# Attention, a soft mixture of experts and an MLP on one core: a conversion that ends sooner, K/Q tiles that later hold weights, and second weights with two rows to a partition

## Chip, cores and metric

The kernel runs on one core of a Trainium2 chip. The metric is device time in microseconds (us), the median of three runs. The core has TensorE (PE, matrix products), VectorE (DVE), ScalarE (ACT), GpSimd (POOL), and SyncE (SP), whose queue issues nearly all DMA transfers.

## What is computed

```python
# q, k, v: (4, 12, 448, 64); x: (1792, 768); float32, w_in and w_out arrive as float64
scores = cap * tanh(q @ k.T / sqrt(64) / cap)          # per batch and head
x = concat_heads(softmax(scores) @ v)                   # (4*448, 768)
logits = x @ phi                                        # 32 slots: 8 experts x 4
d = softmax(logits, axis=tokens); c = softmax(logits, axis=slots)
slot_in = (d.T @ x).reshape(8, 4, 768)
slot_out[e] = relu(slot_in[e] @ w1[e]) @ w2[e]          # w1: (8,768,1024), w2: (8,1024,768)
x = c @ slot_out
h = x @ w_in                                            # (768, 2048)
out = (max(h, 0) + alpha * min(h, 0)) @ w_out           # (2048, 768)
```

## The kernel before

**Three stages in a row.** `attention()` works on 24 pairs of heads (i), four steps each (g = 4i + c): a step computes a chunk of the scores on PE (`qk`), tanh and exp on ACT, and, two steps later, the product with V (`pv`). In the steps with g mod 4 = 1 `pv` ends a pair: ACT copies the PSUM tile o to xu (L413), and the next pair's first V product waits for that copy, since o has one buffer. In the same steps K and Q of the next pair are transposed (`trans_k`, `trans_q`) from the natural K and Q tiles, two buffers of 4 KB a partition in the pools `nat0` and `nat1`. Background work (row sums, normalisation, logits, both softmaxes) is put into later steps by `later`. `softmax_c` runs for each batch once its logits are transposed, the last one behind the loop.

**W_in's conversion** turns float64 into float32 in 24 pieces during attention: one DMA in, one ACT instruction (L184), four on DVE (L185 to L195), one DMA to a scratch tensor. `cv_steps` gives the steps: 4, 7, ... 25, 29 and then every fourth step up to 89. The last piece is stored at step 91, and only then the buffer `cvbuf` (slot 10 of the weight arena) becomes free for weights.

**Expert weights** come as 32 entries in consumption order, four to an expert: two halves of w1 and two of w2, 1.57 MB each. Entries 0 to 9 are loaded into arena slots during attention (steps in `LOADS`), entry 10 into slot 10 after the conversion, entries 11 to 17 in parts into the extra slots (L114), which lie where the attention's pools were, so that each part waits until its predecessor there is free; entry 11 has one part loaded early. Entries 18 and on go into arena slots as the experts leave them (L163). Entries 18, 19, 22, 23, 26, 27, 31, 32 are halves of w2. All loads are issued by SP in this order; w_in's and w_out's follow behind the last expert. A half of w1 is one DMA with 12 KB a row run, one of w2 four DMAs with 3 KB runs.

**The experts stage** (`experts`) does for each expert, on PE: h = slots x w1 (L823; 24 products of 256 columns, four at a time on column groups), two transposes of relu(h) (L837, behind ACT's relu, L834), y += hT x w2 (L845; 24 products of 256 columns, three at a time). An fp32 product shows as two MATMUL records. `build_c` makes the second softmax's operand behind experts 5 and 6, `split_wo(0)` starts w_out's conversion at expert 7 (DVE L185 to L195, L793).

**The MLP stage**: `gather` transposes y (DVE ysb L863), `a_block` multiplies with w_in, `project` does the output products (L954 to L961).

The tile framework keeps data dependences by itself and may place a ready instruction ahead of one that waits, within an engine.

Of the kernel before, what the change touches and what calls it, by code (L numbers as in the profile page):

```python
# [24 lines left out]
def tile_attention_soft_moe_mlp(ctx, tc, q, k, v, cap, phi, w1, w2, w_in, w_out, alpha, out):  # L25
# [29 lines left out]
    LOADS = (2, 4, 6, 8, 10, 12, 14, 16, 18, 20, 21, 22)  # L55
# [16 lines left out]
    c_all = const.tile([P, B, J, NSLOT], F32, name="c_all")  # L72
# [3 lines left out]
    early = [arena.tile([128, SLOT // 4], F32, tag=f"early{c}", name="w") for c in range(QE)]  # L76

# [29 lines left out]

    def load_part(kind, e, i, c, t, after=None):
        if kind == "w2":
            o = 512 * i + 128 * c  # L110
            src = w2[e, o:o + 128, :]
# [121 lines left out]
    def attention():  # L233
        with ExitStack() as pools:
# [3 lines left out]
            nat_0 = pool("nat0")  # L238
            nat_1 = pool("nat1")
# [18 lines left out]
            nat_p, stk_p, v_p, acc_p = (nat_0, nat_1), (stk_0, stk_1), (v_0, v_1), (acc_0, acc_1)  # L258
# [13 lines left out]
            ktails = [nat_p[n].tile([128, 2, D], F32, tag="kt", name="kt") for n in range(2)]  # L272
# [39 lines left out]
            def load(i, names):  # L312
# [3 lines left out]
                for nm in names:  # L316
                    src = {"k": k, "q": q, "v": v}[nm][b, 2 * m:2 * m + 2]

                    if nm == "q":
                        t = nat_p[i % 2].tile([P, J, 2, D], F32, tag=nm, name=nm)  # L320
# [4 lines left out]
                    elif nm == "k":  # L325
                        t = nat_p[i % 2].tile([128, 2 * JK, D], F32, tag=nm, name=nm)
# [264 lines left out]
            def nat_last(ls, fo):  # L591
                ps = aux([P, J * NSLOT], "nd")
                for j in range(J):
                    transpose(
                        ps[:, j * NSLOT:(j + 1) * NSLOT], ls[0:NSLOT, j * P:(j + 1) * P], ident[:NSLOT, :NSLOT]
                    )
                dl[B - 1] = sm_p.tile([P, J, 64], F32, tag="dl", name="dl")
                nc.vector.tensor_copy(out=dl[B - 1][:, :, 0:NSLOT], in_=ps.rearrange("p (j s) -> p j s", j=J))
# [9 lines left out]
            def nat_d(b, ls, fo):  # L608
# [3 lines left out]
                dl[b] = sm_p.tile([P, J, 64], F32, tag="dl", name="dl")  # L612
                nc.vector.tensor_copy(out=dl[b], in_=ps.rearrange("p (j s) -> p j s", j=J))
                later(1, softmax_c, b)
# [30 lines left out]
            def softmax_c(b):  # L645
                lg = dl[b][:, :, NSLOT:2 * NSLOT]
                mx = sm_p.tile([P, J, 1], F32, tag="mx", name="mx")
                sm = sm_p.tile([P, J, 1], F32, tag="sm", name="sm")
                ce = c_all[:, b]
                bc = [P, J, NSLOT]  # L650
                nc.vector.reduce_max(out=mx, in_=lg, axis=AX.X)
                nc.vector.tensor_sub(out=ce, in0=lg, in1=mx.to_broadcast(bc))
# [4 lines left out]
                nc.vector.tensor_mul(out=c_all[:, b], in0=ce, in1=sm.to_broadcast(bc))  # L657

            craw, cout = {}, {}
            cvbuf = slot(NA - 1, [128, 3, 1024], U32, name="cvbuf")  # L660

            def load_w_in(i):
# [4 lines left out]
                nc.sync.dma_start(out=craw[i], in_=w_in[kk * 128:(kk + 1) * 128, fb * 512:(fb + 1) * 512, :])  # L667
# [5 lines left out]
            while len(cv_steps) < ncv:  # L673
                cv_steps.append(cv_steps[-1] + J)
# [39 lines left out]
            for g in range(NPAIR * J + LAG):  # L714
# [4 lines left out]
                if g == 17:  # L719
                    nc.vector.tensor_scalar(out=nalpha_sb, in0=alpha_sb, scalar1=-1.0, scalar2=None, op0=ALU.mult)  # L720
# [5 lines left out]
                run_bg()  # L726
                if i < NPAIR:
# [40 lines left out]
            softmax_c(B - 1)  # L768

    def tail():  # L770
# [27 lines left out]
        def build_c(b, cve_p, ps_w, cstk):  # L798
# [5 lines left out]
            ps = ps_w.tile([128, 512], F32, tag="w", name="tc")[:, :S]  # L804
# [6 lines left out]
        G3 = DM // 256  # L811

        def experts(which, ex2_p, ps_w, yacc, cv_p=None, cstk=None):
            for e in which:
# [4 lines left out]
                h1 = ps_w.tile([128, 512], F32, tag="w", name="h1")[:, :256]  # L819
                for kk in range(KD):  # L820
                    wv = where["w1", e, kk // 3]
                    for j in range(4):
                        nc.tensor.matmul(  # L823
                            h1[32 * j:32 * j + 32, :],
                            slotT[:, kk, :],
                            wv[kk % 3][:, 256 * j:256 * j + 256],
                            start=(kk == 0),
                            stop=(kk == KD - 1),
                            tile_position=(0, 32 * j),
                        )  # L830
                done_with("w1", e, 0)
                done_with("w1", e, 1)
                rl = ex2_p.tile([128, 256], F32, tag="rl", name="rl")
                nc.scalar.activation(out=rl, in_=h1, func=AF.Relu)  # L834
                tp = ps_w.tile([128, 512], F32, tag="w", name="tp")[:, :256]
# [17 lines left out]
                done_with("w2", e, 0)  # L853
                done_with("w2", e, 1)
                if EH <= e < EH + B // 2:
                    for b in (2 * (e - EH), 2 * (e - EH) + 1):
                        build_c(b, cv_p, ps_w, cstk)

        def gather(ps_w, yacc, cv_p, so):
            warm = ps_c.tile([128, 512], F32, tag="c", name="warm")  # L860
            idle(2, warm)
            ysb = cv_p.tile([128, DM], F32, tag="ct", name="ysb")[:32 * G3, :256]
            nc.vector.tensor_copy(out=ysb, in_=yacc[:32 * G3, :256])  # L863
            yt = ps_w.tile([128, 512], F32, tag="w", name="yt")[:, :64 * G3]
            for u in range(2):
                pe[0] = nc.tensor.transpose(
                    yt[:, 32 * G3 * u:32 * G3 * (u + 1)], ysb[:, 128 * u:128 * u + 128], ident[:32 * G3, :32 * G3]
                )
            idle(3, warm)
            for r in range(2):  # L870
                dst = so[:, :, r, :].rearrange("p (g u) s -> p u g s", u=2)
                src = yt.rearrange("p (u g s) -> p u g s", u=2, g=G3)
                nc.vector.tensor_copy(out=dst, in_=src)
# [151 lines left out]
        with (  # L1025
# [3 lines left out]
            with tc.tile_pool(name="ex2", bufs=1, reuse_waits="tile", side="right") as ex2_p:  # L1029
                yacc = ps_c.tile([128, 512], F32, tag="c", name="y")  # L1030
                with tc.tile_pool(name="xtra", bufs=1, reuse_waits="tile") as xt_p:
# [3 lines left out]
                    experts(range(EH), ex2_p, ps_w, yacc)  # L1035
                with (
# [7 lines left out]
                    experts(range(EH, E), ex2_p, ps_w, yacc, cv_p, cstk)  # L1044
# [35 lines left out]
```

## Time and profile before

| what | value |
|---|---|
| median of three runs | 614.9 us (612.85 to 615.34) |
| the profiled execution's own time | 614.49 us |
| its span, first to last instruction | 612.4 us |
| mean granted PE clock | 0.994 |
| busy share of the span | PE 93%, DVE 65%, ACT 52%, POOL 28% |
| moved by DMA | 110.91 MB, mean 181 GB/s |

A span lies between the first and last instruction of the execution; 2.1 us lie around it. "L823" is line 823. PE's busy time comes from modelled ends and is no measure of its rate. Times in the rows count from the span's start.

### The profile page before, as it was taken

To read this page: it belongs to the slowest core of one execution; us is meant where nothing else is said; L and a number is where in the kernel's file an instruction comes from. 1 tells how busy PE (TensorE), PEld (TensorE's weight loads), DVE (VectorE), ACT (ScalarE), POOL (GpSimd) and SP (SyncE) were. 2 spreads that over 40 slices of the span, in tenths; PEclk is the share of its full clock that TensorE was granted. 3 is DMA by queue.
4 is the path that set the end of the run, shared out by engine and by line. 5 is a ranking of instruction groups with operands and counts; after the bars stand their busy time and mean duration, and the time that the engine had idled before them with its cause. 6 is when DMAs were issued, how large, how long until landed. Compare 5 with 4: busy or idle time off the path is not lost.

```text
span 612.4 us, 10754 instructions
## 1 busy us (share of the span) xinstructions
PE 572.0 (93%) x4110; PEld 385.8 (63%) x4110; DVE 395.1 (65%) x734; ACT 318.1 (52%) x509; POOL 168.9 (28%) x158
## 2 busy tenths in 40 slices
PE   6789898999999999989998899999999999999997
PEld 4333444445444545455454668888888888888886
DVE  4497796787668869460023599999566566655552
ACT  4788888888988878620011367665312121221211
POOL 0776777757685765500000000000000000000000
PEclk9899999999999999999999999999999999999999
DMA  4777897887787682799999999000301010010101
GB/s 103 204 213 187 264 270 224 212 249 242 237 214 232 206 244 75 280 381 395 412 408 409 389 409 400 17 1 1 104 1 52 0 45 9 0 52 2 51 1 51
DMA packets 87042, 110.91 MB, mean 181 GB/s; under 512 B 55760, under 2 KB 63440, under 8 KB 85456
## 3 DMA queue, kind: packets, MB, share of 16 engines
q1 hardware_dynamic: 86848, 110.23, 55.1%
q8 instruction: 32, 0.52, 0.3%
q14 instruction: 18, 0.15, 0.1%
q10 hardware_dynamic: 144, 0.00, 0.0%
HBM read 98.41 MB, written 11.80 MB: 180 GB/s over the span
## 4 chain that ended last, share of the span: by engine, by line
PE 69%; ACT 10%; DMA 8%; POOL 6%; DVE 4%; issue 2%; SPq 2%; ACTq 0%; DVEq 0%
PE oc L954 13%; PE oc L960 13%; PE oc L961 13%; PE o L285 6%; PE s L285 5%; DMA w<-in_moe_w_dram 5%; ACT p L388 3%; POOL acc L404 3%; PE y L845 3%; POOL acc L407 3%; PE h L823 3%; ACT p L387 3%; PE hps L909 2%; PE aps L883 2%; PE nx L285 2%
## 5 line engine op out<-in xcount | busy, mean ns | idle before, releaser
L960 PE MATMUL oc<-wsp,gh 128*128 128x512 f32 x448 | 151.7, 339 | 0.0
L954 PE MATMUL oc<-wsp,gh 128*128 128x512 f32 x448 | 151.6, 338 | 0.0
L961 PE MATMUL oc<-wsp,gl 128*128 128x512 f32 x448 | 150.7, 337 | 0.0
L925 ACT ACTIVATE gh<-gf 128x256 fp32r<-128x256 f32 (+1 forms) x96 | 43.5, 453 | 133.0 <-DVE gf L924 127.1
L285 PE MATMUL o<-p,v 128*64 128x448 f32 (+1 forms) x384 | 94.7, 572 | 15.0 <-ACT xu L413 14.9
L387 ACT ACTIVATE p<-s 128x896 f32<-128x896 f32 x96 | 78.9, 822 | 30.9 <-PE s L285 20.2
L388 ACT ACTIVATE p<-p,cap 128x896 f32<-128x896 f32 x96 | 91.1, 950 | 2.2
L954 PEld LDWEIGHTS oc<-wsp,gh 128*128 128x128 f32 x448 | 85.0, 190 | 10.7 <-issue 0.9
L961 PEld LDWEIGHTS oc<-wsp,gl 128*128 128x128 f32 x448 | 84.7, 189 | 11.1 <-issue 1.2
L960 PEld LDWEIGHTS oc<-wsp,gh 128*128 128x128 f32 x448 | 85.0, 190 | 9.7 <-issue 0.4
L404 POOL TENSOR_TENSOR acc<-p 128x448 f32<-128x448 f32 x48 | 58.6, 1241 | 73.0 <-ACT p L388 73.0
L926 DVE TENSOR_TENSOR gl<-gf,gh 128x256 fp32r<-128x256 f32 (+1 forms) x96 | 44.9, 468 | 45.0 <-ACT gh L925 44.9
L285 PEld LDWEIGHTS s<-qh,kh 64*128 64x128 f32 (+1 forms) x168 | 18.2, 187 | 67.6 <-issue 27.3
L921 DVE TENSOR_SCALAR mn<-hps,alpha 128x256 f32<-128x256 f32 (+1 forms) x81 | 39.5, 487 | 24.0 <-PE hps L909 23.9
L411 POOL TENSOR_TENSOR acc<-acc,p 128x448 f32<-128x448 f32 x46 | 53.8, 1190 | 1.8
L407 POOL TENSOR_TENSOR acc<-acc,p 64x448 f32<-64x448 f32 x46 | 53.7, 1168 | 1.7
L285 PE MATMUL s<-qh,kh 64*128 64x448 f32 (+1 forms) x168 | 46.0, 477 | 0.0
L285 PEld LDWEIGHTS o<-p,v 128*64 128x64 f32 (+1 forms) x384 | 19.0, 134 | 40.1 <-ACT xu L413 21.6
L924 DVE SCALAR_TENSOR_TENSOR gf<-hps,mn 128x256 f32<-128x256 f32 (+1 forms) x81 | 34.6, 427 | 2.7
L285 PE MATMUL s<-qh,kl 64*128 64x448 f32 (+1 forms) x168 | 35.5, 367 | 0.0
L285 PE MATMUL s<-ql,kh 64*128 64x448 f32 (+1 forms) x168 | 35.4, 367 | 0.0
L845 PE MATMUL y<-w,hT 128*32 128x256 f32 x384 | 30.3, 381 | 2.1 <-DMA w<-in_moe_w_dram 1.1
(151 smaller groups left out, 767.1 us busy)
## 6 DMA issues: line engine op xcount, KB each, us to landing
w<-in_moe_w_dram SPq DMA_DIRECT2D x64, 384.0 KB, 7.8
w<-in_moe_w_dram SPq DMA_DIRECT2D x12, 1536.0 KB, 10.0
cvbuf<-in_moe_w_in_dram SPq DMA_DIRECT2D x24, 512.0 KB, 5.1
w<-in_moe_w_out_dram SPq DMA_DIRECT2D x16, 768.0 KB, 8.9
w_in<-cvbuf SPq DMA_DIRECT2D x24, 256.0 KB, 2.4
w<-in_moe_w_dram SPq DMA_DIRECT2D x12, 512.0 KB, 6.6
q<-in_q_dram SPq DMA_DIRECT2D x48, 112.0 KB, 4.0
k<-in_k_dram SPq DMA_DIRECT2D x48, 96.0 KB, 4.9
```

The source lines that it names most:

```text
L285: ins = nc.tensor.matmul(*a, **kw)
L387: nc.scalar.activation(out=pe, in_=ps[:, :n, :S], func=AF.Tanh)
L388: nc.scalar.activation(out=pe, in_=pe, func=AF.Exp, scale=cap_sb)
L404: nc.gpsimd.tensor_add(out=a[:, u, :], in0=pt[i, 0][:, u, :], in1=pe[:, u, :])
L407: nc.gpsimd.tensor_add(out=a[r, u, :], in0=a[r, u, :], in1=pt[i, JK][r, 0, :])
L411: nc.gpsimd.tensor_add(out=a[:, u, :], in0=a[:, u, :], in1=pe[:, u, :])
L845: pe[0] = nc.tensor.matmul(yacc[32 * g:32 * g + 32, :256], hT[:, kk % 2, kk // 2, :], wv[kk % 4][:, 256 * g:256 * g + 256], start=(e == 0 ...
L925: nc.scalar.activation(out=gh, in_=gf, func=AF.Copy)
L926: nc.vector.tensor_sub(out=gl, in0=gf, in1=gh)
L954: ins = nc.tensor.matmul(o, gh[:, ts], wo_h[f][:, cols], start=(f == 0 and not second), stop=False)
L960: nc.tensor.matmul(o, gh[:, ts], wo_l[f][:, cols], start=False, stop=False)
L961: nc.tensor.matmul(o, gl[:, ts], wo_h[f][:, cols], start=False, stop=(f == KF - 1 and not more))
```

## The change

1. `cv_steps`: from step 29 the spacing alternates 4, 3, so that the last piece is at step 82 and slot 10 is free from step 84. `LOADS` has 19, 20, 21 in place of 20, 21, 22. W_in's rows are permuted; two of six pieces take two DMAs.
2. Natural K, Q and K's tail lie in two tiles of the arena (`nats`) in place of the pools; after the last two pairs' transposes each takes a 512 KB part of entry 12 (w1 of expert 3) at steps 86 and 90. The extra slots are 8 KB smaller.
3. w2 rows: partition p holds rows 2p and 2p+1 of a block of 256, so a DMA has 6 KB runs and a half takes two DMAs; relu(h) is interleaved to match.
4. y in four column groups of 192 in place of three of 256; `hidden_e(e + 1)` is written ahead of expert e's transposes and y; tp and tc use other PSUM buffers; `gather` follows.
5. `softmax_c` once for all batches behind the loop; `dl` in one constant tile; nalpha there too.

```diff
-    LOADS = (2, 4, 6, 8, 10, 12, 14, 16, 18, 20, 21, 22)
+    LOADS = (2, 4, 6, 8, 10, 12, 14, 16, 18, 19, 20, 21)
...
+    nats = [arena.tile([128, FE], F32, tag=f"nat{n}", name="nat") for n in range(2)]
...
+    def w2_rows(e, i):
+        return w2[e, 512 * i:512 * i + 512, :].rearrange("(j p u) f -> p j u f", p=128, u=2)
...
+    def load_nat(c):
+        key = loads[NA + 1]
+        where.setdefault(key, []).append(load_part(*key, c, nats[c]))
...
-            src = w2[e, 512 * i:512 * i + 512, :].rearrange("(k p) f -> p k f", p=128)
+            src = w2_rows(e, i)
...
-        parts = [(t[:, c], src[:, c]) for c in range(t.shape[1])]
         if kind == "w1":
             parts = [(t, src)]
+        elif kind == "w2":
+            parts = [(t[:, 2 * j:2 * j + 2], src[:, j]) for j in range(2)]
+        else:
+            parts = [(t[:, c], src[:, c]) for c in range(t.shape[1])]
...
-                later(1, softmax_c, b)
...
-                cv_steps.append(cv_steps[-1] + J)
+                cv_steps.append(cv_steps[-1] + (J if len(cv_steps) % 2 else J - 1))
...
                 run_bg()
+                if i >= NPAIR - 3 and i < NPAIR - 1 and c == 2:
+                    load_nat(i - NPAIR + 3)
...
-            softmax_c(B - 1)
+            softmax_c()
+            nc.vector.tensor_scalar(out=nalpha_sb, in0=alpha_sb, scalar1=-1.0, scalar2=None, op0=ALU.mult)
...
+        def hidden_e(e, ps_w, kks):
+            if e == E:
+                return
+            if kks.start == 0:
+                h1s[e] = ps_w.tile([128, 512], F32, tag="w", name="h1")[:, :256]
+            for kk in kks:
+                wv = where["w1", e, kk // 3]
+                for j in range(4):
+                    nc.tensor.matmul(
+                        h1s[e][32 * j:32 * j + 32, :],
+                        slotT[:, kk, :],
+                        wv[kk % 3][:, 256 * j:256 * j + 256],
+                        start=(kk == 0), stop=(kk == KD - 1), tile_position=(0, 32 * j),
+                    )
+                if kk % 3 == 2:
+                    done_with("w1", e, kk // 3)
...
+                if e == 0:
+                    hidden_e(0, ps_w, range(0, KD))
...
+                hidden_e(e + 1, ps_w, range(0, 3))
...
+                hidden_e(e + 1, ps_w, range(3, KD))
                 for kk in range(KE):
                     wv = where["w2", e, kk // 4]
-                    for g in range(G3):
+                    for g in range(4):
                         pe[0] = nc.tensor.matmul(
-                            yacc[32 * g:32 * g + 32, :256],
+                            yacc[32 * g:32 * g + 32, :GC],
...
-                            wv[kk % 4][:, 256 * g:256 * g + 256],
+                            wv[kk % 4][:, GC * g:GC * g + GC],
...
-            nc.vector.tensor_copy(out=ysb, in_=yacc[:32 * G3, :256])
+            nc.vector.tensor_copy(out=ysb[:, :GC], in_=yacc[:, :GC])
+            nc.scalar.activation(out=ysb[:, GC:], in_=yacc[:, 128:GC], func=AF.Copy)
```

`GC` is 192. `softmax_c` itself does the same operations as before on all four batches (112 partitions x 512 elements) in place.

## Rows read from the trace of the kernel before

**Rows 1.** Stages: us, busy us of PE, PEld, DVE, ACT, POOL, clock, DMA.

```profile
276.00:341.00 65.00, 57.56 (x802) 32.03 (x801) 10.72 (x30) 6.30 (x18) 2.18 (x7) 1.00 1.02 405
349.00:612.40 263.40, 258.76 (x1510) 222.95 (x1510) 181.49 (x351) 94.57 (x188) 0.00 (x0) 1.00 0.21 74
```

**Rows 2.** Chain of work that ended last, 250 to 350 us: start, us, what.

```profile
276.22 2.77 PE h L823 x48
...
332.55 7.85 DMA w<-in_moe_w_dram
...
340.44 0.63 PE y L845 x6
```

**Rows 3.** Timeline of PE in the experts stage: start, us, instructions [idle before <-releaser].

```profile
302.16 0.44 PE L837 MATMUL tp<-ident,rl 128*128 128x128 f32 x2 [0.56 <-ACT rl L834]
302.95 3.44 PE L845 MATMUL y<-w,hT 128*32 128x256 f32 x45 [0.35 <-DVE hT L838]
...
309.77 0.44 PE L837 MATMUL tp<-ident,rl 128*128 128x128 f32 x2 [0.57 <-ACT rl L834]
...
332.58 1.50 PE L823 MATMUL h<-w,slotT 128*32 128x256 f32 x24 [0.54 <-DMA w<-in_moe_w_dram]
```

**Rows 4.** Timeline of SP, 236 to 285 us: its DMA issues.

```profile
249.85 28.00 SPq L114 DMA_DIRECT2D w<-in_moe_w_dram  x23
```

**Rows 5.** Windows around the end of attention, columns as in Rows 1.

```profile
236.00:248.00 12.00, 12.00 (x96) 6.36 (x92) 10.52 (x15) 10.21 (x15) 9.09 (x8) 1.00 0.14 43
248.00:273.40 25.40, 22.59 (x197) 11.41 (x195) 13.70 (x27) 11.46 (x18) 5.65 (x6) 1.00 0.96 360
```

**Rows 6.** Waits of SP, 248 to 278 us: total us, times, longest.

```profile
SPq L114 <- PE ss L285: 3.5, 1, 3.5
...
SPq L114 <- DVE c_all L657: 1.7, 1, 1.7
```

**Rows 7.** DMA issued at 268.99 us: KB, us to landing.

```profile
w<-in_moe_w_dram SPq DMA_DIRECT2D x1, 512.0 KB, 6.9
```

**Rows 8.** Windows of 2 us where the experts' loads begin, columns as above.

```profile
274.00:276.00 2.00, 1.65 (x10) 1.54 (x10) 0.88 (x4) 0.31 (x1) 0.00 (x0) 1.00 0.94 307
...
280.00:282.00 2.00, 2.00 (x28) 1.55 (x29) 0.12 (x1) 0.00 (x0) 0.00 (x0) 1.00 0.97 287
```

**Rows 9.** Windows of 3 KB runs (w2), then 6 KB runs (w_out); last column GB/s.

```profile
299.00:304.00 5.00, 4.09 (x65) 2.13 (x56) 0.19 (x1) 0.38 (x1) 0.31 (x1) 1.00 1.03 399
354.00:358.00 4.00, 4.00 (x22) 1.54 (x18) 4.00 (x7) 2.39 (x4) 0.00 (x0) 1.00 1.02 418
```

**Rows 10.** Windows of the attention's loop.

```profile
124.00:252.00 128.00, 123.11 (x903) 61.80 (x902) 99.45 (x174) 107.44 (x152) 83.39 (x73) 1.00 0.72 208
```

**Rows 11.** Timeline of ACT at the end of a pair.

```profile
196.71 0.67 ACT L184 ACTIVATE cvbuf<-cvbuf 128x512 f32<-128x512 f32 x1
197.27 0.55 ACT L413 ACTIVATE xu<-o 128x448 f32<-128x448 f32 x1
```

**Rows 12.** DVE groups in the last 9 us of attention: busy us, mean ns.

```profile
L652 DVE TENSOR_TENSOR c_all<-dl,mx 112x128 f32<-112x128 f32 x1 | 0.3, 292 | 0.0
```

**Rows 13.** Windows of 2 us around an idle stretch of PE, and a later one.

```profile
22.00:24.00 2.00, 0.43 (x6) 0.06 (x2) 1.82 (x2) 2.00 (x5) 1.95 (x2) 1.00 1.07 238
24.00:26.00 2.00, 1.00 (x4) 0.29 (x4) 2.00 (x5) 1.97 (x4) 0.00 (x0) 0.72 0.59 132
26.00:28.00 2.00, 2.00 (x10) 0.83 (x6) 1.22 (x3) 0.83 (x1) 1.10 (x2) 0.50 0.56 161
...
270.00:272.00 2.00, 0.89 (x17) 0.74 (x21) 0.86 (x5) 1.44 (x4) 0.00 (x0) 1.00 1.02 396
```

**Rows 14.** Timeline of DVE at the last expert and behind it.

```profile
329.04 0.55 DVE L185 TENSOR_SCALAR ct<-ct 128x768 f32<-128x768 f32 x1
...
333.13 0.96 DVE L793 TENSOR_TENSOR wsp<-ct,wsp 128x768 fp32r<-128x768 f32 x1 [0.96 <-ACT wsp L792]
...
341.13 0.42 DVE L863 COPY ysb<-y 96x256 f32<-96x256 f32 x1 [5.46 <-PE y L845]
```

More of the change, by code (lines that the diff above doesn't have):

```diff
@@ L71, in tile_attention_soft_moe_mlp @@
     lomask, spare = masks[:, 0:1], masks[:, 1:2]
-    c_all = const.tile([P, B, J, NSLOT], F32, name="c_all")
+    dl_all = const.tile([P, B, J, 2 * NSLOT], F32, name="c_all")
+    c_all = dl_all[:, :, :, NSLOT:]
     slotT = const.tile([128, KD, NSLOT], F32, name="slotT")
@@ L269, in head @@
                 return slice(64 * u, 64 * u + 64)
-            ktails = [nat_p[n].tile([128, 2, D], F32, tag="kt", name="kt") for n in range(2)]
+            nat_q = [t[:P, 0:2 * S // P * D].rearrange("p (j h d) -> p j h d", j=J, h=2) for t in nats]
+            nat_k = [t[:, 512:512 + 2 * JK * D].rearrange("p (j d) -> p j d", d=D) for t in nats]
+            ktails = [t[:, 512 + 2 * JK * D:].rearrange("p (h d) -> p h d", h=2) for t in nats]
             for t in ktails:
@@ L319, in load @@
                     if nm == "q":
-                        t = nat_p[i % 2].tile([P, J, 2, D], F32, tag=nm, name=nm)
+                        t = nat_q[i % 2]
                         for h in range(2):
@@ L325, in load @@
                     elif nm == "k":
-                        t = nat_p[i % 2].tile([128, 2 * JK, D], F32, tag=nm, name=nm)
+                        t = nat_k[i % 2]
                         by_j = t[:, :2 * JK, :].rearrange("p (j h) d -> p j h d", h=2)
@@ L643, in slot_sums, with softmax_c @@
                     nc.vector.tensor_copy(out=r, in_=ps)
[L645 to L652, printed above, removed]
+            def softmax_c():
+                ce = c_all.rearrange("p b j s -> p (b j) s")
+                mx = const.tile([P, B * J, 1], F32, name="mx")
+                sm = const.tile([P, B * J, 1], F32, name="sm")
+                bc = [P, B * J, NSLOT]
+                nc.vector.reduce_max(out=mx, in_=ce, axis=AX.X)
+                nc.vector.tensor_sub(out=ce, in0=ce, in1=mx.to_broadcast(bc))
                 nc.scalar.activation(out=ce, in_=ce, func=AF.Exp)
@@ L656, in softmax_c, with w_in_rows @@
                 nc.vector.reciprocal(out=sm, in_=sm)
-                nc.vector.tensor_mul(out=c_all[:, b], in0=ce, in1=sm.to_broadcast(bc))
+                nc.vector.tensor_mul(out=ce, in0=ce, in1=sm.to_broadcast(bc))
             craw, cout = {}, {}
             cvbuf = slot(NA - 1, [128, 3, 1024], U32, name="cvbuf")
+            def w_in_rows(kk):
+                w = DM // 4
+                if kk < 4:
+                    return [(0, 128, w * kk)]
+                return [(64 * u, 64, w * (2 * (kk - 4) + u) + 128) for u in range(2)]
             def load_w_in(i):
@@ L666, in load_w_in @@
                 craw[i] = cvbuf[:, i % 2].rearrange("p (f t) -> p f t", t=2)
-                nc.sync.dma_start(out=craw[i], in_=w_in[kk * 128:(kk + 1) * 128, fb * 512:(fb + 1) * 512, :])
+                for p, n, row in w_in_rows(kk):
+                    nc.sync.dma_start(out=craw[i][p:p + n], in_=w_in[row:row + n, fb * 512:(fb + 1) * 512, :])
             ncv = KD * (DFF // 512)
@@ L809, in build_c, with experts @@
             nc.vector.tensor_copy(out=cstk[:, b * S:(b + 1) * S], in_=ps)
-        G3 = DM // 256
-        def experts(which, ex2_p, ps_w, yacc, cv_p=None, cstk=None):
+        GC = DM // 4
+        h1s = {}
+        def hidden_e(e, ps_w, kks):
[10 more added lines that the diff above has]
+                        wv[kk % 3][:, 256 * j:256 * j + 256],
+                        start=(kk == 0),
+                        stop=(kk == KD - 1),
+                        tile_position=(0, 32 * j),
+                    )
+                if kk % 3 == 2:
+                    done_with("w1", e, kk // 3)
+        def experts(which, ex2_p, ps_w, ps_c, yacc, cv_p=None, cstk=None):
             for e in which:
@@ L818, in experts @@
                 nc.gpsimd.memset(hT, 0.0)
[L819 to L832, printed above, removed]
-                rl = ex2_p.tile([128, 256], F32, tag="rl", name="rl")
-                nc.scalar.activation(out=rl, in_=h1, func=AF.Relu)
-                tp = ps_w.tile([128, 512], F32, tag="w", name="tp")[:, :256]
+                if e == 0:
+                    hidden_e(0, ps_w, range(0, KD))
+                rl = ex2_p.tile([128, 256], F32, tag="rl", name="rl")
+                nc.scalar.activation(
+                    out=rl.rearrange("q (u p) -> q p u", u=2),
+                    in_=h1s[e].rearrange("q (p u) -> q p u", u=2),
+                    func=AF.Relu,
+                )
+                hidden_e(e + 1, ps_w, range(0, 3))
+                tp = ps_c.tile([128, 512], F32, tag="c", name="tp")[:, :256]
                 for u in range(2):
@@ L1034, in tail @@
                     load_free()
-                    experts(range(EH), ex2_p, ps_w, yacc)
+                    experts(range(EH), ex2_p, ps_w, ps_c, yacc)
                 with (
@@ L1043, in tail @@
                     cstk = ex_p.tile([128, NT], F32R, name="cstk")
-                    experts(range(EH, E), ex2_p, ps_w, yacc, cv_p, cstk)
+                    experts(range(EH, E), ex2_p, ps_w, ps_c, yacc, cv_p, cstk)
                     gather(ps_w, yacc, cv_p, so)
```

40 lines of the change are left out of this document (18 added, 22 removed).

## The prediction

> **What bounds the kernel now.** I read the stages first, then the chain, then for each stage the wait that ends last.
>
> The last stage is the longest: from 349 us to the end PE is busy for 258.8 of 263.4 us while DMA moves 74 GB/s [rows 1]. It is PE's own rate; no line of its project loop is in the diff, so it moves as a block with its start. The stages ahead decide.
>
> In the experts stage DMA moves 405 GB/s at a share of 1.02 over all of 276 to 341 us, and PE is busy for 57.6 of 65 us [rows 1]. Both are near their end, so the reader must ask which arrives last. PE takes 309.77 - 302.16 = 7.61 us an expert, with two waits inside: 0.57 us for relu ahead of the transposes and 0.35 us for the copy to hT [rows 3]. From 276.22 eight of these give 337.1 us. The chain, however, runs through a weight load that lands at 332.55 + 7.85 = 340.40 us, and six products of y follow it in 0.63 us [rows 2]; PE's first wait for a load is at 332 us [rows 3]. So both are close, and DMA is the later by some 3 us. A gain in PE alone buys nothing beyond this; a gain in DMA buys at most what it takes from 340.40.
>
> Why does DMA end there? Ahead of the stage it has a hole, 43 GB/s from 236 to 248 us, for want of free buffers; then it moves 360 GB/s [rows 5]. In that stretch SP issues 23 parts for the extra slots over 28 us [rows 4], because each waits for an attention buffer; the last long wait, 3.5 us for the slot sums, ends at about 273.4 us [rows 6]. Did DMA still have work queued then? The part issued at 268.99 landed 6.9 us later, at 275.9 [rows 7], and yet 274 to 276 us shows only 307 GB/s, and 280 to 282 us only 287 [rows 8]. I read it so: the queue had just run dry when the parts of 273.4 us came. From there on it is full.
>
> **The change part by part.**
>
> *Loads into the hole.* Entry 10 (1.57 MB) is issued at step 87 in place of 91, and 1.05 MB of entry 12 at steps 86 and 90. At some 2.7 us a step (step 91 stands right ahead of 249.85 us [rows 4]) this is the hole of [rows 5], where SP has little queued; behind the new parts stand only the last V loads. At 405 GB/s the 2.62 MB are 6.5 us. But this is credit with a queue that ran dry at 273.4 us anyway: whatever is moved earlier only makes DMA wait longer for the slot sums. What comes after 273.4 us, the parts of entries 16 and 17 and entries 18 to 32, is the same bytes. The credit is worth 6.5 us if the queue was full at 273.4, nothing if it was empty; [rows 8] say nearly empty, while the landing at 275.9 says that some of the 16 engines still worked. I take -0.4 us.
>
> *The c softmax behind the loop.* The last extra part waited 1.7 us for c_all [rows 6]; now dl lies in a constant tile, and the part waits for the slot inputs only. The dip at 280 to 282 us [rows 8] is (405 - 287) x 2 us = 0.24 MB or 0.6 us; I take -0.4, bounds 0 and -0.6. Inside the loop three softmaxes leave DVE and ACT, behind it one of four times the size comes. Its 128-element subtraction took 0.29 us [rows 12]; four such steps at four times this are under 5 us of DVE, from 276.5 us on. hT of expert 0 waits for DVE until about 281 us, at most 2 us; PE's slack (next part) hides this.
>
> *PE's work per expert.* y has 16 passes; a pass now has 192 columns in place of 256, so 3.4 us [rows 3] become about 2.6. With h of the next expert ahead of them the two waits (0.92 us) can be filled. 7.61 - 0.85 - 0.92 = 5.84 us an expert, and eight end at 276.2 + 46.7 = 323 us, the transposes of c on top. The weights land 15 us later. So all of this is hidden behind DMA, and is worth only that PE no longer adds to the end. If DMA were not there, it would be worth 14 us.
>
> *6 KB runs.* Eight of the entries from 18 on are halves of w2, 12.58 MB. In the trace 3 KB runs move at 399 GB/s and 6 KB runs, those of w_out, at 418 [rows 9]: 31.5 us become 30.1, -1.4 us, straight from the end. Bounds: 0, if the rate of [rows 9] is set by what PE does beside it, and -1.4. The Trainium skill, DMA: Bandwidth & Descriptors, Why small descriptors are slow, has a fixed overhead of about three cycles for a packet beside 32 bytes a cycle; worked out from it, 3 KB to 6 KB would be an estimated 1.5% of 31.5 us, 0.5 us; the rows show three times that.
>
> *The last arrival.* The last DMA now carries two of the eight kk instead of one. Behind it come 16 narrower records' worth, 4 passes of 0.16 us and the tail, against 0.63 us [rows 2]: +0.2. In `gather` DVE's copy of 0.42 us [rows 14] has 192 columns and ACT makes a second one beside it: -0.1, and the ACT copies to so end behind the first k's of `a_block`, which hide them; without this cover they cost up to 0.5.
>
> *Attention.* Sixteen conversions from step 29 on stand today at steps with g mod 4 = 1, so that ACT's 0.67 us stands ahead of xu [rows 11], for which PE's next V product waits. With spacings of 4 and 3 four of sixteen stay there; the others go to steps with full chunks, where tanh and exp fill ACT more. DVE gets 15 conversions over 53 steps instead of 60, and loses three softmaxes. PE's whole idle time from 124 to 252 us is 128 - 123.1 = 4.9 us [rows 10], which bounds a gain; a loss is bounded by the twelve moved ACT instructions in front of p, at most 12 x 0.67 = 8 us, though ACT is idle for 20 of 128 us there, which makes most of it free. SP gets 8 more DMA issues. I take -0.6, and from -2.5 to +1.5 as what is plausible. The end of attention also moves the slot sums, so this counts in full.
>
> *PE's clock.* From about 300 us on PE will wait for loads most of the time: per half of w1, 1.57 MB in 3.8 us, it has 24 records, 1.5 us of work [rows 3]; per DMA of w2, 0.79 MB in 1.9 us, 0.64 us. At 22 to 24 us PE stood still for most of the time, and the granted clock fell to its lower level, 1.2 GHz: 0.72 in the mean of the next 2 us and 0.50 in those after them; at 270 to 272 us PE also stood still for more than a half and kept 1.00, 2.4 GHz [rows 13]. Which of the two the new waits will resemble, the rows don't say. A fall costs what these windows lost, (0.28 + 0.50) x 2 = 1.6 us, if it falls on the last products, the gather or the first of the MLP; I take +0.5. The Trainium skill, TensorE: Matmul & The Clock Gate, Loop structure matters more than you think, names exactly this pattern, a DMA wait between bursts of products, as the one in which the clock drops. By that rule the whole 1.6 would be paid; the rows leave it open.
>
> *The rest* (nalpha, PSUM buffers, permuted rows of w_in) is beside idle DVE and ACT in the experts stage and costs nothing; the longest, nalpha, would otherwise delay the first hT by its own length.
>
> Sum: -0.4 - 0.4 - 1.4 + 0.2 - 0.1 - 0.6 + 0.5 = -2.2 us. The profiled execution took 614.49 us for a span of 612.4; the sum gives 612.3 for it. The median, 614.9, is 0.4 higher: 612.7 us. Half a per cent, about what a measurement of this kernel tells from no change, is 3.1 us.
>
> **Rivals.**
>
> *The queue was full.* If DMA was still behind at 273.4 us, all the credit counts: -6.5 - 1.4 and the small terms give 607 us; PE's 323 us leaves room for it. For: 360 GB/s and a share of 0.96 from 248 us on [rows 5], the landing at 275.9 [rows 7]. Against: both dips [rows 8]. If attention gains its 4 us, the time is similar, 609. 22%.
>
> *The clock eats it.* The experts end 2.7 us earlier, but at half clock, and the MLP starts at most 1 us earlier: 614 us, no change. 18%.
>
> *An order that blocks.* h of expert e + 1 is written ahead of y of expert e. PE takes its instructions in order; if h(7) is put ahead of y(6), PE waits for w1 of expert 7, landing at about 331 us, with y(6) and the transposes of c behind it. DVE waits for these with `split_wo(0)` behind, which took from 329.04 to 334.09 us [rows 14], and hT(7) behind that. 331 + 1.5 (h) + 2.6 (y) + 1.5 (transposes, copies) + 5.1 + 0.6 (hT) + 2.6 (y) = 344.9, 3.8 us later than 341.1: 618 us with the gain in attention. It decides when those end behind 338 us, the last landing. For: today the first products of h stand ahead of y in experts 0 to 2. Against: from expert 3 on, where weights come late, PE goes straight from tp to y [rows 3]. With an attention slowed by the moved conversions: 12%.
>
> **Chances.** Forecast 48%, around 612.7 us, of its own from 610.5 to 614.5. Full queue or a quicker attention 22%, clock 18%, slower 12%. Faster by over 0.5% (below 611.8): nearly all of the 22% and a seventh of the forecast's 48%, 0.29. Slower (above 618): 0.10. The rest, 0.61. For eight in ten the range takes the forecast, the clock, and half of each of the others: 608.3 to 617.5.
>
> **What would show it.** The last w2 load lands at 337 to 338.5 us; windows of w2 at 415 GB/s or more; 236 to 248 us filled, and in its place a thinner DMA between 250 and 273 us (this decides against the first rival); PE with waits for loads from some 300 us on, and then its clock; L413 without L184 in front. Wrong would be the forecast if the last load landed before 335 us, if y(7) came late for another reason than a load, or if attention ended 2 us away from today's end.

## The result, and the profile after

The changed kernel took 622.92 us in the median (620.53 to 626.33, 4 runs), the kernel before 615.12 (612.85 to 616.14, 4 runs) measured with it: a ratio of 1.0142, 95% interval 1.0112 to 1.0173. It is slower by 1.4%, and outside the range. The profiled span is 618.7 us against 612.4, so 6.3 us have to be found. Windows of the changed kernel, columns as in [rows 1]:

```profile
124.00:252.00 128.00, 117.31 (x853) 58.62 (x857) 99.79 (x148) 100.31 (x141) 81.35 (x68) 1.00 0.76 223
236.00:248.00 12.00, 10.97 (x91) 6.04 (x91) 7.46 (x11) 9.33 (x14) 7.61 (x8) 1.00 0.58 207
248.00:281.00 33.00, 30.19 (x261) 15.09 (x257) 16.60 (x33) 17.53 (x26) 9.90 (x9) 1.00 0.66 231
...
284.00:346.00 62.00, 52.96 (x922) 32.84 (x925) 12.54 (x31) 8.91 (x19) 2.49 (x8) 0.91 1.02 417
```

Its chain of work that ended last, 300 to 358 us (start, us, what):

```profile
326.73 18.74 DMA w<-in_moe_w_dram
...
345.51 1.09 PE y L878 x16
```

The start of the copy xu of pair 22, ACT's timeline, in the kernel before and then in the changed one:

```profile
252.38 0.52 ACT L413 ACTIVATE xu<-o 128x448 f32<-128x448 f32 x1
```

```profile
259.99 0.53 ACT L426 ACTIVATE xu<-o 128x448 f32<-128x448 f32 x1
```

This makes a table by stage. All lengths are from the two profiled executions.

| from, to | before | after | difference |
|---|---|---|---|
| start to xu of pair 22 | 252.4 | 260.0 | +7.6 |
| xu to the first product of h | 23.7 | 24.3 | +0.6 |
| first h to the end of y | 65.0 | 62.3 | -2.7 |
| end of y to the first product oc of the MLP | 7.8 | 9.6 | +1.8 |
| first oc to the end | 263.5 | 262.5 | -1.0 |

The experts did what was forecast: DMA moves 417 GB/s in place of 405 [rows 1], and the stage is 2.7 us shorter. But it begins 8 us late. In 128 us of the attention's loop PE is busy for 117.31 us where it was busy for 123.11 [rows 10]: the loss sits there. 236 to 248 us now moves 207 GB/s instead of 43 [rows 5], and 248 to 281 us 231 instead of 360: the loads were moved into the hole, and what followed became thinner, down to 51 GB/s from 256 to 264 us.

What does PE wait for in attention? Its waits from 76 to 262 us (total us, times, longest), in the changed kernel:

```profile
PE o L298 <- ACT xu L426: 6.8, 8, 1.6
PE nx L298 <- DVE kl L366: 2.4, 2, 2.2
PE lr L298 <- DVE xn L507: 2.3, 1, 2.3
PE nx L298 <- DVE s_run L653: 1.9, 1, 1.9
```

and the first in the kernel before, where kl is 1.4 us and xn and s_run are not in the list:

```profile
PE o L285 <- ACT xu L413: 7.3, 10, 1.5
```

The wait for ACT's xu, which the prediction weighed, has not grown. The new ones are for DVE (beside one of 0.8 us for a natural K tile's load). So look at DVE's instructions of W_in's conversion, 76 to 276 us (count | busy us, mean ns | idle before), first before, then after:

```profile
L195 DVE SCALAR_TENSOR_TENSOR cvbuf<-cvbuf 128x512 uint32<-128x512 uint32 x17 | 16.1, 949 | 0.4
...
L192 DVE SCALAR_TENSOR_TENSOR cvbuf<-cvbuf 128x512 uint32<-128x512 uint32 x17 | 11.8, 691 | 0.5
...
L189 DVE TENSOR_SCALAR cvbuf<-cvbuf 128x512 uint32<-128x512 uint32 x17 | 7.2, 425 | 0.5
L185 DVE TENSOR_SCALAR cvbuf<-cvbuf 128x512 f32<-128x512 f32 x17 | 7.1, 416 | 0.1
```

```profile
L208 DVE SCALAR_TENSOR_TENSOR cvbuf<-cvbuf 128x512 uint32<-128x512 uint32 x17 | 19.1, 1124 | 0.5
L205 DVE SCALAR_TENSOR_TENSOR cvbuf<-cvbuf 128x512 uint32<-128x512 uint32 x17 | 16.3, 959 | 0.6
L202 DVE TENSOR_SCALAR cvbuf<-cvbuf 128x512 uint32<-128x512 uint32 x17 | 14.9, 875 | 0.5
...
L198 DVE TENSOR_SCALAR cvbuf<-cvbuf 128x512 f32<-128x512 f32 x17 | 11.4, 671 | 4.7 <-ACT cvbuf L197 4.5
```

The same 17 pieces, the same operations and sizes: 61.7 us in place of 42.2. One piece shows why. The timeline of the kernel before (DVE, POOL):

```profile
199.78 2.24 POOL L404 TENSOR_TENSOR acc<-p 128x448 f32<-128x448 f32 x2 [2.25 <-ACT p L388]
...
207.96 0.43 DVE L189 TENSOR_SCALAR cvbuf<-cvbuf 128x512 uint32<-128x512 uint32 x1
...
208.42 0.69 DVE L192 SCALAR_TENSOR_TENSOR cvbuf<-cvbuf 128x512 uint32<-128x512 uint32 x1
...
209.54 1.77 POOL L404 TENSOR_TENSOR acc<-p 128x448 f32<-128x448 f32 x1 [2.73 <-ACT p L388]
...
209.63 0.68 DVE L195 SCALAR_TENSOR_TENSOR cvbuf<-cvbuf 128x512 uint32<-128x512 uint32 x1
```

and of the changed one:

```profile
214.86 3.16 POOL L417 TENSOR_TENSOR acc<-p 128x448 f32<-128x448 f32 x2 [2.92 <-ACT p L401]
...
215.78 1.25 DVE L202 TENSOR_SCALAR cvbuf<-cvbuf 128x512 uint32<-128x512 uint32 x1
...
217.06 1.51 DVE L205 SCALAR_TENSOR_TENSOR cvbuf<-cvbuf 128x512 uint32<-128x512 uint32 x1
...
217.99 3.12 POOL L420 TENSOR_TENSOR acc<-acc,p 64x448 f32<-64x448 f32 x2
...
218.61 1.50 DVE L208 SCALAR_TENSOR_TENSOR cvbuf<-cvbuf 128x512 uint32<-128x512 uint32 x1
...
220.03 0.47 DVE L653 SCALAR_TENSOR_TENSOR s_run<-s_run,fo,ss 128x256 f32<-128x256 f32 x1
...
220.56 0.65 PE L298 MATMUL nx<-ident,xn 128*112 128x128 f32 x4 [1.86 <-DVE s_run L653]
```

POOL adds up the row sums of a pair in six additions, about 7 us, and then rests; in the kernel before for 2.25 to 5.81 us in the pairs from 195 to 256 us. Before, the piece stands in that rest (POOL idle for 2.73 us ahead of 209.54) and its four instructions take 2.2 us. After, it stands beside the additions: the same instructions take 0.41, 1.25, 1.51 and 1.50 us, POOL's first two additions 3.16 us in place of 2.24, and s_run, in DVE's order behind the piece, keeps PE waiting for 1.86 us. A step with g mod 4 = 1 is where the rest lies, and from step 29 on every piece of the kernel before had such a step.

The two take turns. Taken singly, POOL's four additions in this stretch end at 216.74, 218.02, 219.56 and 221.10 us, and DVE's L202, L205 and L208 at 217.03, 218.57 and 220.11. Behind each end on DVE the next one on POOL follows after 0.99 us; behind POOL's first three the next one on DVE after 0.29, 0.55 and 0.55 us, in step with their lengths alone (0.43, 0.69 and 0.68). So it looks as if one engine's instruction runs while the other's waits.

The Trainium skill has a rule on this that the prediction passed over: SBUF — State Buffer, SBUF: two separate sides, says that DVE and GpSimd share one pair of SBUF ports, and that for a DVE instruction in a two-port mode or with two SBUF inputs it is an exclusive lock: whichever instruction starts first has it to its end, and the other blocks. The turns agree with a lock. One thing does not fit by the recorded starts: L198 begins 0.48 us behind the addition of 214.86 us and is not slowed (0.41 us), while that addition takes 1.88 us. That it is these ports which are shared, no run here shows.

**The theory**: the conversion's new steps leave POOL's rest, and this costs the 7.6 us. **Rivals**: the pieces lie closer together (53 steps in place of 60); ACT's instructions ahead of xu; natural K and Q in two tiles, loaded later; something in the experts.

### The profile page after: what moved, and what is told of

Read it like the earlier page. It is cut to its first block, busy times and chain, and to the rows that moved or that the text cites. A ratio compares the mean times of both kernels' runs of the same rounds, so it can differ in the third digit from the quotient of the medians.

```text
span 618.7 us, 10969 instructions
## 1 busy us (share of the span) xinstructions
PE 569.5 (92%) x4238; PEld 387.7 (63%) x4238; DVE 407.0 (66%) x716; ACT 319.9 (52%) x511; POOL 174.7 (28%) x158
## 4 chain that ended last, share of the span: by engine, by line
PE 51%; DVE 17%; DMA 12%; ACT 8%; POOL 5%; issue 4%; SPq 1%; ACTq 0%; DVEq 0%
PE oc L989 10%; PE oc L995 10%; PE oc L996 10%; DMA w<-in_moe_w_dram 8%; PE o L298 5%; PE s L298 5%; POOL acc L417 3%; ACT p L400 3%; ACT p L401 2%; POOL acc L420 2%; DVE cvbuf L205 2%; DVE cvbuf L208 2%; PE hps L944 2%; DVE ct L205 2%; PE nx L298 1%
## 5 line engine op out<-in xcount | busy, mean ns | idle before, releaser
L424 POOL TENSOR_TENSOR acc<-acc,p 128x448 f32<-128x448 f32 x46 | 57.6, 1274 | 1.8
L298 PE MATMUL tr<-ident,nat 128*128 128x128 f32 (+1 forms) x192 | 25.2, 272 | 6.5 <-DMA nat<-in_k_dram 5.3
```

Source lines behind the costliest of these rows:

```text
L298: ins = nc.tensor.matmul(*a, **kw)
L424: nc.gpsimd.tensor_add(out=a[:, u, :], in0=a[:, u, :], in1=pe[:, u, :])
```

## Experiments

**The changed kernel with the old steps.**

```diff
-    LOADS = (2, 4, 6, 8, 10, 12, 14, 16, 18, 19, 20, 21)
+    LOADS = (2, 4, 6, 8, 10, 12, 14, 16, 18, 20, 21, 22)
-                cv_steps.append(cv_steps[-1] + (J if len(cv_steps) % 2 else J - 1))
+                cv_steps.append(cv_steps[-1] + J)
```

> The changed kernel with the old steps of the conversion (every fourth step to 89) and the old loading steps, all else as changed. Theory (port): the conversion's DVE instructions got slower because they now run beside POOL's additions, and PE waits for DVE; then attention ends as before (first h product at about 276 to 277 us instead of 284.3), the conversion's last two instructions take about 0.7 and 0.9 us in the mean, and the time falls by 6 to 8 us to 614 to 617. Rival (tiles): the natural K and Q in arena tiles, or the softmax moved behind the loop, delay attention; then the first h product stays at 282 us or later and the time at 620 or more.

615.39 us, ratio to the kernel before 1.0021 (0.9995 to 1.0048). Xu of pair 22 starts at 252.0 us, and among PE's waits (76 to 262 us) kl is back at 1.4 us and xn and s_run are gone. The steps cost everything that the change lost, and the natural tiles cost nothing that shows. But with the old steps nothing is won either: h to the end of y takes 62.1 us (before 65.0), and 2.8 us go again between y and the MLP, 10.6 us in place of 7.8.

**The kernel before with the new steps**: the same two edits, the other way round.

> The kernel before with the new steps of the conversion (ending at 82) and the new loading steps alone. Theory (port): attention ends 6 to 8 us later than before, as in the changed kernel, and the time is 621 to 624 us. Rival (tiles): attention ends within 1.5 us of before and the time stays at 614 to 616.

630.7 us, ratio 1.0271 (1.0249 to 1.0292); xu of pair 22 at 263.7 us. The steps alone are enough. They cost 11.3 us of attention here, 8.0 in the changed kernel (260.0 against 252.0), whose loop has three softmaxes fewer; whether that is why, no run tests.

**The kernel before with the old spacing, two steps earlier.**

```diff
-            cv_steps = [4, 7, 10, 13, 16, 19, 22, 25, 29]
+            cv_steps = [4, 7, 10, 13, 16, 19, 22, 25, 27]
```

> The kernel before with the conversion from step 27 to 87 at every fourth step, so with the same spacing but g mod 4 = 3 in place of 1. Theory (port): every piece then stands beside POOL's additions; DVE takes 4.5 to 5.5 us for a piece in place of 2.2, and the kernel is slower by 8 us or more, 623 or later. Rival (density): it is the closer spacing that costs, not the phase; then this kernel takes 613 to 617 us.

633.24 us, ratio 1.0303 (1.0268 to 1.0339), xu at 271.7 us. Its conversion on DVE, 76 to 276 us:

```profile
L192 DVE SCALAR_TENSOR_TENSOR cvbuf<-cvbuf 128x512 uint32<-128x512 uint32 x17 | 21.7, 1279 | 0.4
L195 DVE SCALAR_TENSOR_TENSOR cvbuf<-cvbuf 128x512 uint32<-128x512 uint32 x17 | 20.6, 1209 | 0.3
L189 DVE TENSOR_SCALAR cvbuf<-cvbuf 128x512 uint32<-128x512 uint32 x17 | 18.8, 1105 | 0.5
L185 DVE TENSOR_SCALAR cvbuf<-cvbuf 128x512 f32<-128x512 f32 x17 | 14.2, 834 | 1.7 <-ACT cvbuf L184 1.7
```

With the same distance of four steps and another remainder the pieces take 75.3 us in place of 42.2. It is the place within the pair, not the density.

**Both kernels without most of POOL's additions.** In both, two of the three kinds of additions are left out:

```diff
-                        if i < NPAIR - 1:
-                            nc.gpsimd.tensor_add(out=a[r, u, :], in0=a[r, u, :], in1=pt[i, JK][r, 0, :])
...
-                    if i < NPAIR - 1:
-                        for u in range(2):
-                            nc.gpsimd.tensor_add(out=a[:, u, :], in0=a[:, u, :], in1=pe[:, u, :])
```

> The changed kernel without two of POOL's three kinds of additions to the row sums (the tail chunk and the last chunk are left out of the sums, so the normalisation is another one). Theory (port): POOL is busy for some 2.5 us a pair in place of 7, the conversion's pieces of DVE fall to 2.2 to 3 us at any step, and attention ends 6 us or more earlier than in the changed kernel. Rival (order): DVE is late because of where the pieces stand among its other work; then pieces and attention stay within 2 us of the changed kernel.

> Control to e4: the kernel before without two of POOL's three kinds of additions to the row sums (the sums then lack those chunks). If the contention of the conversions with POOL is what the new steps cost, little is to be gained here: the sixteen conversions from step 29 on already stand in POOL's gap, and xu of pair 22 starts at 251 to 252.4 us. If POOL's additions cost attention time in any kernel, it starts as much earlier as in e4 against the changed kernel, by nearly 10 us, at about 243 us.

Changed kernel: 610.91 us in one run, xu of pair 22 at 250.2 us, 9.8 us earlier than with the additions. Kernel before: 613.02 us, xu at 250.6, earlier by 1.8. In the changed kernel without the additions L205 takes 692 ns in the mean, with them 959.

Without most of POOL's additions beside them the two kernels end attention 0.4 us apart, the changed one first; with them 7.6. The same conversion steps, the same ACT instructions: only additions of POOL were taken away. PE's waits for xn and s_run are gone too.

How firm is this, with one profiled execution of each? Four runs with the changed kernel's attention and the old steps (the first experiment and the three on the start of the MLP, below) have xu of pair 22 at 250.2 to 255.3 us. All that scatters lies ahead of pair 10. From xu of pair 10 to that of pair 22 the kernel before takes 125.9 us, the other complete kernels whose pieces stand in POOL's rest 125.8 to 126.0; the changed kernel takes 131.9, the kernel before with the new steps 137.9, the one at the other remainder 143.0, and the two without the additions 124.8 (changed) and 125.3. So 6.0 us of the loss are clear of scatter, and they go with POOL's additions. This is the cause of the loss. The loading steps, which moved with the conversion's, are not: the last experiment has both early, its pieces in the rest, and takes 125.8.

By which way it reaches PE is not split. Beside PE's waits for DVE, ACT's waits for POOL's additions ahead of p grew from 5.7 to 8.9 us in all (76 us to the end of attention).

**6 KB runs alone**, in the kernel before (y stays in three groups of 256):

```diff
-            src = w2[e, 512 * i:512 * i + 512, :].rearrange("(k p) f -> p k f", p=128)
+            src = w2_rows(e, i)
...
-                nc.scalar.activation(out=rl, in_=h1, func=AF.Relu)
+                nc.scalar.activation(
+                    out=rl.rearrange("q (u p) -> q p u", u=2),
+                    in_=h1.rearrange("q (p u) -> q p u", u=2), func=AF.Relu)
```

> The kernel before, in which only w2 is loaded with two rows to a partition: 6 KB runs, two DMAs a half in place of four, and relu's output interleaved to match. The conversions, the gather and the order of h and y stay. If longer runs are what shortened the experts' loads, the last w2 lands some 1.4 us ahead of 340.4 us, PE ends y at about 339.7 to 340 us, and the time is 613.5 to 614, at the edge of what can be measured. If it was the rest (narrower y, loads moved ahead), the last landing stays at 340.4 us and the time is that of the kernel before.

616.37 us, ratio 1.0028 (1.0009 to 1.0046): nothing won. All of PE's waits from 296 to 347 us:

```profile
PE tp L847 <- ACT rl L840: 4.8, 6, 0.8
PE y L855 <- DVE hT L848: 1.1, 3, 0.4
```

No wait for a load is left: h to the end of y takes 65.3 us, and PE sets it. The loads came earlier, but in the kernel before PE's waits for loads were only 1.6 us in all (296 to 347 us), and the edit costs PE time of its own: the interleaved relu takes ACT 0.61 us in place of 0.38, so that PE waits for it 0.79 us an expert in place of 0.57, some 1.8 us in eight. In this execution the granted clock also lay at 0.50 over the first products of h (48 records in 4.01 us, before 2.80). That the longer runs pay together with the narrower y is concluded from this; no run has the narrower y alone.

**The start of the MLP.** Three runs on the changed kernel with the old steps: first with the gather's copies on DVE and W_o's second split behind the second `a_block`, then with the copies alone, then with idle products in the waits of the last two experts.

```diff
-            nc.scalar.activation(out=ysb[:, GC:], in_=yacc[:, 128:GC], func=AF.Copy)
+            nc.vector.tensor_copy(out=ysb[:, GC:], in_=yacc[:, 128:GC])
...
-            for r in range(2):
-                nc.vector.tensor_copy(out=so[:, 0:4, r, :], in_=yt[:, 0:128].rearrange(rows, g=4))
-                ...
-                    nc.scalar.activation(out=so[64 * u:64 * u + 64, 4:6, r, :], in_=src, func=AF.Copy)
+            nc.vector.tensor_copy(out=so[:, 0:4], in_=src.to_broadcast([128, 4, 2, NSLOT]))
+            for u in range(2):
+                ...
+                nc.vector.tensor_copy(out=so[64 * u:64 * u + 64, 4:6], in_=src.to_broadcast([64, 2, 2, NSLOT]))
...
-            split_wo(1, cv_p)
             a_block(0, 0, 128)
...
             a_block(0, 256, 128)
+            split_wo(1, cv_p)
```

> The changed kernel with the old steps of the conversions and loads (e1), in which all copies of the gather are on DVE, each to both r at once, and the second part of W_o is split behind the second a_block. e1 took 10.6 us from the last y to the first product of the MLP against 7.8 before. If that is the gather's copies and the split's place, this falls to 8 to 9 us and the time to 612 to 613.5. If it is PE's clock, the stretch stays above 10 us and the time at e1's 615.

> e1 with the gather's copies on DVE alone; the second part of W_o is split at the changed place, ahead of the first a_block. If the gather's two engines cost the start of the MLP, the stretch from the last y to its first product falls from 10.6 to some 8 us, as in e6. If it is the split's place, it stays at 10 us, and e6 gained by the split alone.

> e1 with idle products (results not used) added in the waits of the last two experts, so that PE does not stand still ahead of the gather. If half clock is what the start of the MLP loses, the granted clock stays at 1.0 through 340 to 352 us, the stretch from the last y to the first product of the MLP falls by some 1 us, and the time to about 614.3. If the clock is a side matter, or the added products delay y, it stays at 615 or more.

Copies and split: 614.49 us, ratio 1.0002 (0.9985 to 1.0019), y to oc 7.9 us. Copies alone: 614.41 us, ratio 1.0003 (0.9987 to 1.0019), also 7.9. So the copies do it; where the split is written makes no difference that can be measured. The time fell less than the stretch, and not to the 612 to 613.5 us expected: attention ended 2 to 3 us later than in the first experiment (xu of pair 22 at 255.3 and 254.0 us), lost between pairs 8 and 10 for a reason that no run shows. The gather in the changed kernel, timelines of DVE and ACT:

```profile
347.72 0.29 DVE L904 COPY so<-yt 128x128 f32<-128x128 f32 x1 [0.68 <-PE yt L900]
348.04 0.45 ACT L908 ACTIVATE so<-yt 64x64 f32<-64x64 f32 x2 [0.74 <-DVE so L904]
348.52 0.29 DVE L904 COPY so<-yt 128x128 f32<-128x128 f32 x1 [0.51 <-ACT so L908]
348.85 0.45 ACT L908 ACTIVATE so<-yt 64x64 f32<-64x64 f32 x2 [0.36 <-DVE so L904]
...
350.53 0.27 ACT L932 ACTIVATE a_stk<-aps 64x128 fp32r<-64x128 f32 x1 [1.24 <-issue]
350.70 0.91 ACT L197 ACTIVATE ct<-w 128x768 f32<-128x768 f32 x1
...
351.64 0.27 ACT L932 ACTIVATE a_stk<-aps 64x128 fp32r<-64x128 f32 x1
...
353.40 0.50 PE L944 MATMUL hps<-cstk,a_stk 128*128 128x512 f32 x1 [1.19 <-DVE a_stk L933]
```

and with the copies on DVE:

```profile
341.88 0.42 DVE L904 COPY so<-yt 128x256 f32<-128x256 f32 x1 [0.42 <-PE yt L900]
342.23 0.58 DVE L907 COPY so<-yt 64x128 f32<-64x128 f32 x2
...
344.35 0.27 ACT L931 ACTIVATE a_stk<-aps 64x128 fp32r<-64x128 f32 x1 [8.37 <-DMA w<-w_in]
...
344.97 0.27 ACT L931 ACTIVATE a_stk<-aps 64x128 fp32r<-64x128 f32 x1 [0.35 <-DVE a_stk L932]
...
345.15 0.89 ACT L197 ACTIVATE ct<-w 128x768 f32<-128x768 f32 x1
```

DVE and ACT copy out of yt by turns: in the trace each waits for the other, and the six copies take 1.6 us where DVE's three take 0.9; and in the changed kernel ACT's 0.91 us of the split stands between its two copies of a_stk, so that PE's hps waits. With the gather off ACT, the split falls behind both.

Idle products: 628.02 us, ratio 1.0205 (1.017 to 1.024). They were no free filling, and they changed the order: the edit ties each idle product to the one of h or y ahead of it, and h of expert 7 now stands ahead of expert 6's transposes and y. PE's timeline:

```profile
326.88 2.79 PE L846 MATMUL h<-w,slotT 128*32 128x256 f32 x24 [9.52 <-DMA w<-in_moe_w_dram]
```

PE stands still for 9.52 us with that work behind it, and from the last h to the end of y 15.8 us go by, against 6.9 without them. On the clock the run says less than was hoped: it stays at 1.0 from 331 to 358 us, but falls under the last aps (24 records in 2.83 us in place of 1.53), inside y to oc, which takes 11.6 us. In the first experiment such a fall is 1.0 of its 10.6 us. So the clock is a part of what lengthens that stretch there, and in neither run most of it.

**The early end, inside POOL's rest.** The kernel with the gather on DVE and the late split, with the conversion ended at step 81 and the changed `LOADS`:

```diff
-            cv_steps = [4, 7, 10, 13, 16, 19, 22, 25, 29]
+            cv_steps = [4, 7, 9, 11, 13, 15, 17, 19, 21, 25, 29]
```

> e6 with the conversion ended at step 81 and the loads at the changed steps 79, 83 and 87, but with every piece from step 21 on at a step of the form 4k + 1, in POOL's gap; the pieces that no longer find such a step lie closer together before step 21. If the loss of the change is the phase of its steps and not their early end, attention ends as in e1 and e6 (xu of pair 22 at 252 to 255 us, some 2 us more if the crowded early pieces cost). If DMA had work queued ahead of the slot sums (the rival of the full queue), the loads made earlier then count for up to 6.5 us: 608 to 610. If the queue was dry, as the forecast had it, the time is e6's, 614 to 615.

619.63 us, ratio 1.0081 (1.0062 to 1.0099). From step 29 on its pieces take 2.2 to 3.2 us each, and from xu of pair 8 to that of pair 22 it needs 147.0 us, like the kernel before (147.2; changed kernel 156.6). But the crowded pieces ahead of it lie beside POOL: xu of pair 8 comes at 111.9 us in place of 105.2, far more than the 2 us allowed for. Behind attention nothing is won that stands out: from xu of pair 22 to the end it takes 360.2 us, and with the same gather and the old steps 361.0 (with the late split) and 358.3 (with the copies alone). By the end of attention these are one entry apart (entry 10 at step 87 in place of 91; entry 12's parts stand early in all three): 1.57 MB, or 3.9 us at 405 GB/s, if the queue had been full.

No version that computes the whole result beat the kernel before.

## Why the prediction was wrong

**Attention: the step that failed.** The term was -0.6 us, with bounds -2.5 and +1.5. It measured +7.6, 6.0 of it from pair 10 on; an end of attention 2 us away was the forecast's own sign of being wrong. The working bounded a loss by twelve ACT instructions in front of p, found ACT idle often enough, and noted of DVE only how many pieces stand in how many steps, as if a piece cost the same anywhere. DVE's price depends on what POOL does: 2.2 us in its rest, up to 5.5 us beside its additions. The runs without POOL's additions show it as the cause (7.6 us between the kernels become -0.4), the run with the old spacing at another remainder that density is not. No rival had it as a mechanism; the 12% of the last one only took in "an attention slowed by the moved conversions", without a price. The trace of before had the evidence, in its early pieces, which stand at all remainders. L192, 5 to 80 us:

```profile
L192 DVE SCALAR_TENSOR_TENSOR cvbuf<-cvbuf 128x512 uint32<-128x512 uint32 x8 | 8.0, 1000 | 0.2
```

From 76 us on L192 takes 691 ns in the mean. One operation of one size with two means is a question, and it was not asked.

**Loads into the hole: -0.4, right at nothing.** The hole was filled and the stretch behind it became thinner (51 GB/s from 256 to 264 us), which was named as what decides against the full queue; the last experiment has no clear gain from it.

**6 KB runs and the experts: right in sum, -2.7 where -2.0 was summed** (runs -1.4, last arrival +0.2, c's softmax and credit -0.4 each). The parts were not measured singly. With 6 KB runs alone DMA moves 413 GB/s over 282 to 342 us, in the kernel before 407 over 281 to 341: 1.5%, or some 0.9 us of 60, an estimate, where -1.4 was taken. A window of 5 us in the changed kernel, beside h and y:

```profile
299.00:304.00 5.00, 5.00 (x102) 3.18 (x98) 0.19 (x1) 0.50 (x1) 0.31 (x1) 1.00 0.99 412
```

**PE's work per expert: right for the first experts, wrong for the others, without harm.** 5.84 us were worked out, so that PE would wait from 300 us on. In the changed kernel the transposes of experts 0, 1 and 2 (290.11, 295.81, 301.50 us) follow each other after 5.7 us, with the waits for relu and hT filled. From expert 4 on h of the next expert no longer stands ahead of them, and PE waits 0.79 and 0.35 us. Timeline of PE in the changed kernel:

```profile
319.45 0.44 PE L869 MATMUL tp<-ident,rl 128*128 128x128 f32 x2 [0.79 <-ACT rl L861]
...
327.10 0.44 PE L869 MATMUL tp<-ident,rl 128*128 128x128 f32 x2 [0.79 <-ACT rl L861]
...
334.23 1.50 PE L841 MATMUL h<-w,slotT 128*32 128x256 f32 x24 [2.86 <-DMA w<-in_moe_w_dram]
337.92 1.57 PE L841 MATMUL h<-w,slotT 128*32 128x256 f32 x24 [2.19 <-DMA w<-in_moe_w_dram]
```

An expert takes 7.65 us there with the transposes of c, 6.97 without (312.48 to 319.45 us), and the first wait for a load comes at 331.4 us, 47 us behind the first h, not 24. That DMA was what ended last held with little to spare: with 6 KB runs alone no wait for a load is left.

**The last arrival and the gather: +0.1 in sum, measured +1.8 in the changed kernel.** ACT's copies were taken to run beside DVE's and behind the first products of `a_block`. They alternate with DVE's (from y to the first aps 2.3 us, before 1.7), and push W_o's split between the copies of a_stk (+1.1 us).

**PE's clock: +0.5, measured some +0.2.** It falls, behind the two waits of 2.86 and 2.19 us, to 0.50 from 339.2 to 346.0 us; one window of it, in the changed kernel:

```profile
340.00:342.00 2.00, 1.39 (x14) 0.74 (x18) 0.19 (x1) 0.20 (x1) 0.00 (x0) 0.50 1.04 427
```

The Trainium skill, TensorE: Matmul & The Clock Gate, Loop structure matters more than you think, names waits for DMA between bursts of products as what costs the clock, and the trace agrees. Of the slow stretch (0.50 is the lower level, 1.2 GHz) most lies ahead of the last load, where PE would have waited anyway; the last 16 records of y take 1.09 us against 0.86 at full clock (copies alone on DVE), so it cost some 0.2 us. A second fall was not foreseen: PE was busy for 0.57 us of 276 to 278 and 1.27 us of 278 to 280, and the clock is 0.50 from 282 to 288 us, over the first products of h (72 records in 5.93 us; at full clock 24 take 1.50). PE's later waits for loads, 5.05 us, take that in. With the old steps it fell on an `aps` instead (2.55 us in place of 1.53) and cost 1.0.

**The order that blocks** did not come in the changed kernel: y of expert 6 stands ahead of the wait for expert 7's w1. The run with idle products has it, with PE's wait of 9.52 us, so the rival's mechanism is real.

What stays open: the first product of h comes 0.6 us later behind xu than before (part of that stretch is at half clock), and the MLP is 1.0 us shorter; neither was looked into.

## What to carry to other kernels

When work moves to another place in a loop, price it with what runs there on each engine that it may share something with, not by its mean and its own engine's idle share; if one operation of one size has two durations in the trace, find out what separates them before trusting either. A regular step number (every fourth, always the same remainder) may be what keeps two engines apart. And a gain in loads is a gain only as far as the next engine has slack: work that one out with its waits in it.

## What was not expected of the hardware

A 128x512 DVE instruction of 0.43 us took 1.25 us beside POOL's additions, one of 0.69 us 1.5, and two additions of POOL 3.16 us in place of 2.24: both engines lose at once. Between 76 and 276 us DVE's 17 pieces grew by 19.5 us (61.7 - 42.2), and the end of attention moved by 7.6, although DVE was busy for under 80% of the loop [rows 10]. It moved in a few places: of the 6.0 us lost from pair 10 on 5.4 lie between the starts of xu of pairs 15 and 17 and of pairs 18 and 19. The latter two are 16.0 us apart in place of 13.0, and s_run's wait shown above lies between them.
